# Attention and two MoE layers on one core: operand addresses of the seven products, the order of the raw w_out loads, and which blocks are split on chip

## The chip, the cores and the metric

One core of one Trainium2 chip. The metric is the device time of one execution in microseconds (us), the median over runs. In what follows PE is TensorE (matrix products), PEld its weight loads, DVE is VectorE, ACT is ScalarE, POOL is GpSimd, and SP is SyncE, the engine that issues all DMAs here, in the order of the program.

## The reference, cut to what matters

```python
def _attn_ref(q, k, v, p):              # 8 batches, 8 heads, 576 tokens, 64 columns; p: 32 pack tokens
    p_packed = sm_attn(p, k, v)
    return sm_attn(q, p_packed, p_packed)

def _moe_ref(x, w_gate, w_val, w_out, rms_g):        # 4608 tokens, 512 -> 1536 -> 512
    xn = x / np.sqrt(np.mean(x * x, axis=-1, keepdims=True) + 1e-06) * rms_g
    g = xn @ w_gate
    return (g * (1.0 / (1.0 + np.exp(-g))) * (xn @ w_val)) @ w_out

def _moe2_ref(x, w_in, w_out, alpha):                # 4608 tokens, 512 -> 2048 -> 512
    h = x @ w_in
    return (np.maximum(h, 0.0) + alpha * np.minimum(h, 0.0)) @ w_out
```

The three run one after the other: the output of attention, with the heads side by side, is the x of the first layer, and its output is the x of the second. All tensors are float32.

## The kernel before

Every float32 operand of the large products is split into two parts that TensorE takes at its full rate (fp32r): a high part, made by ACT (`split_hi`, L109), and a low part, the rest, made by DVE (`split_lo`, L112). A product is then three matmuls into the same accumulator (`mm3`, L120 to L123): weights high by moving high (L121), weights high by moving low (L122), weights low by moving high (L123).

The program has two large stages. Until about 940 us, attention and the first layer run in 12 chunks of tokens; the first layer's result goes to y_dram in DRAM. From there on the second layer runs in five groups (`PAIRS`), of widths w = 512, 512, 512, 384 and 384, each covering 2w tokens. The change is to this stage, apart from two of its addresses.

In the second layer, the 2 x 2 block product of tokens by w_in is done with seven products instead of eight. The moving operands are sums and differences of quarters of y, named b11, t1, t2, t4, t3, b21, b22; `prep` (L769) makes them for the next group, in tiles `yh` and `yl` of the pool `p2`. The weights are seven tiles per step, w7, each with a high and a low half. In group 1 they are made on chip (`make_w7`, L824, with ACT and POOL, from raw blocks i2_raw) and stored to w7_dram; groups 2 to 5 load them (`load_w7`, L819, DMA at L822).

A group goes like this:

- Eight steps (the loop over i). Step i has the seven products of six matmuls each. ACT copies the first out as m1 (L1133, a tile `th`), DVE adds the others to it (`add2`, L1033, tiles `tl` and `th`) and applies the PReLU. Then `second` is called for two of the four results, those of the first half of the tokens: hidden blocks i and i + 8. The other two are kept as g2.
- `second` splits the activation into hh and hl, and the w_out block of 128 x 512 into in_h and in_l, by ACT and DVE; then it puts a function that issues the block's matmuls into the list `fill`, from where they are taken later, between the products of the next step. The raw w_out blocks i and i + 8 come from w_dram by one DMA of 512 KB (`load_o2`, L1046 to L1052) into one of two tiles o2_raw, one for even i and one for odd. So the load for step i + 2 can start when DVE has made in_l of block i + 8 of step i. In group 1 the in_h, in_l of blocks 0 to 7 (e = 0) are also stored to os_dram (L1073).
- The deferred loop (over j = 0 to 15), for the second half of the tokens: `second` takes the kept g2, in the order of blocks 0, 8, 1, 9, and so on. Blocks 0 to 7 (j even, `again` and e = 0) are not split: in_h and in_l are loaded from os_dram (L1067). Blocks 8 to 15 (j odd) are split from o2_raw, which is loaded for them with 256 KB each. At j = 2, `results` (L1090) copies the sums of the first half out by ACT and DVE and stores them (DMA at L1101).
- The `results` of the second half are called at the end of step 0 of the next group.

All engines take their instructions in program order, and so does SP with its DMAs: a DMA that has to wait for its tile, or for an evacuation, holds back all DMAs behind it. The w7 tiles of four of the seven products and the in_h, in_l tiles share 12 places of the pool `wa`. In the names of the profile the numbers are dropped, and w7_dram and w_dram both read `w_dram`; a w7 tile is `w`, o2_raw is `o_raw`, i2_raw is `i_raw`.

At L1116 to L1120 a step of before begins (after group 1) with the loads of the weights for the next step, and then with its own raw w_out load:

```python
                elif i + 1 < NP2:
                    load_w7(k_ + 1, EARLY + ORDER)
                elif pr + 1 < len(PAIRS):
                    load_w7(k_ + 1, EARLY)
                load_o2(i)
```

Of the kernel before, what the change touches and what calls it, by code (L numbers as in the profile page):

```python
# [8 lines left out]
F32 = mybir.dt.float32  # L9
# [9 lines left out]
def attention_moe_moe2_kernel(ctx, tc, q, k, v, p, w_gate, w_val, w_out, rms_g, w_in2, w_out2, alpha, out):  # L19
    nc = tc.nc  # L20
# [8 lines left out]
    NF2 = FF2 // 128  # L29
# [5 lines left out]
    NJ = NF // 2  # L35
# [6 lines left out]
    NP2 = NF2 // 2  # L42
    PAIRS, t0_ = [], 0
# [44 lines left out]
    one = ctx.enter_context(tc.tile_pool(name="one", bufs=1))  # L88
    wg1 = ctx.enter_context(tc.tile_pool(name="wg1", bufs=NWG1))
    ps = ctx.enter_context(tc.tile_pool(name="ps", bufs=1, space=bass.MemoryType.PSUM))  # L90
    y_dram = tc.dram_tile([KD, 128, NT], F32, name="y_dram")
    w7_dram = tc.dram_tile([NP2 * 7, 128, 2, 256], F32, name="w7_dram")
    os_dram = tc.dram_tile([NP2, 2, 128, 512], F32, name="os_dram")
    w_dram = tc.dram_tile([2 * NF2, 128, 4, 128], F32, name="w_dram")
    gv_dram = tc.dram_tile([NJ * 4, 128, 512], F32, name="gv_dram")

    ident = const.tile([128, 128], F32, name="ident")
    g_col = const.tile([128, HG], F32, name="g_col")
# [9 lines left out]
    def split_hi(hi, src):  # L108
        nc.scalar.activation(out=hi, in_=src, func=ACTF.Copy)  # L109

    def split_lo(lo, src, hi):
        nc.vector.tensor_tensor(out=lo, in0=src, in1=hi.bitcast(F32), op=ALU.subtract)  # L112
# [7 lines left out]
    def mm3(o, lh, ll, rh, rl, first, last, more=False):  # L120
        nc.tensor.matmul(out=o, lhsT=lh, rhs=rh, start=first, stop=False, skip_group_check=more)  # L121
        nc.tensor.matmul(out=o, lhsT=lh, rhs=rl, start=False, stop=False, skip_group_check=more)  # L122
        nc.tensor.matmul(out=o, lhsT=ll, rhs=rh, start=False, stop=last, skip_group_check=more)  # L123

    with tc.manual_schedule():
# [685 lines left out]
        def new_w7(k_, which):  # L811
            for n in which:
                if n in EARLY:
                    t = one.tile([128, 2, 256], F32R, tag="gv", name="w7", bufs=8)
                else:
                    t = wa.tile([128, 2, 256], F32R, tag="w", name="w7")
                w7[k_, n] = t
# [6 lines left out]
        def make_w7(i):  # L824
            new_w7(i, EARLY + ORDER)
            blocks = []
            for e in range(2):
                t = one.tile([128, 2, 256], F32, tag="s7", name="i2_raw", bufs=2)
                nc.sync.dma_start(
                    out=t.rearrange("p h x -> p (h x)"),  # L830
                    in_=w_dram[2 * (i + e * NP2)].rearrange("p c x -> p (c x)"),
                )
                blocks += [t[:, 0], t[:, 1]]
            a11, a12, a21, a22 = blocks

            def product(n, src):
                t = w7[i, n]
                split_hi(t[:, 0], src)
                nc.gpsimd.tensor_tensor(out=t[:, 1], in0=src, in1=t[:, 0].bitcast(F32), op=ALU.subtract)
                nc.sync.dma_start(out=w7_dram[i * 7 + n], in_=t.bitcast(F32))  # L840

            def combine(out, x, y, op):
                nc.gpsimd.tensor_tensor(out=out, in0=x, in1=y, op=op)

            yield
            product(0, a11)
            product(1, a12)
            product(3, a22)
            combine(a22, a21, a22, ALU.add)
            yield  # L850
            combine(a21, a11, a21, ALU.subtract)
            product(4, a22)
            combine(a11, a22, a11, ALU.subtract)
            yield
            product(6, a21)
            combine(a12, a12, a11, ALU.subtract)
            yield
            product(5, a11)
            product(2, a12)
# [5 lines left out]
        for c, (t0, n, cuts) in enumerate(CH):  # L865
# [148 lines left out]
            if c == NP1 - 2:  # L1014
                ap_ctx.close()
                p2 = ctx.enter_context(tc.tile_pool(name="p2", bufs=1, side="right", reuse_waits="tile"))
# [29 lines left out]
        def load_o2(i, e0=0):  # L1046
            x = "hl"[i % 2]
            t = one.tile([128, 2, T], F32, tag="x" + x, name="o2_raw")
            nc.sync.dma_start(
                out=t[:, e0:2], in_=o2_pair[i, 1, e0:2].rearrange("e p x -> p e x")  # L1050
            )
            o2[i] = t  # L1052
# [3 lines left out]
        def second(g, f, w, acc, first, last, keep=False, again=False):  # L1056
            n_h[0] += 1
            hh, hl = [
                ring.tile([128, T], F32R, tag="ho"[n_h[0] % 2] + x, name="h" + x, bufs=2)[:, 0:w] for x in "hl"
            ]  # L1060
            split_hi(hh, g)
            split_lo(hl, g, hh)
            oh, ol = [wa.tile([128, T], F32R, tag="w", name="in_" + x) for x in "hl"]
            e, i = divmod(f, NP2)
            if again and e == 0:
                for x, t in enumerate((oh, ol)):
                    nc.sync.dma_start(out=t.bitcast(F32), in_=os_dram[i, x])  # L1067
            else:
                split_hi(oh, o2[i][:, e])
                split_lo(ol, o2[i][:, e], oh)  # L1070
            if keep and e == 0:
                for x, t in enumerate((oh, ol)):
                    nc.sync.dma_start(out=os_dram[i, x], in_=t.bitcast(F32))  # L1073

            def block():
                for t in range(w // 128):
                    cs = slice(t * 128, (t + 1) * 128)
                    mm3(acc(t), hh[:, cs], hl[:, cs], oh, ol, first, last)
            fill.append(block)
# [23 lines left out]
                    )  # L1103

        finish = None
        making = make_w7(1)
        next(making)
        for pr, (t0, w) in enumerate(PAIRS):
            odd = pr % 2
            acc1, acc2 = accumulators(1 - odd), accumulators(odd)  # L1110
            g2 = {}
            for i in range(NP2):
                k_ = pr * NP2 + i
                if pr == 0 and i + 1 < NP2:
                    pass
                elif i + 1 < NP2:  # L1116
                    load_w7(k_ + 1, EARLY + ORDER)
                elif pr + 1 < len(PAIRS):
                    load_w7(k_ + 1, EARLY)
                load_o2(i)  # L1120
                if i == NP2 - 2 and pr + 1 < len(PAIRS):
                    y_rows.append(load_rows(pr + 1, 0))

# [45 lines left out]
                    finish()  # L1169
                    finish = None  # L1170
            prepare = prep(pr + 1) if pr + 1 < len(PAIRS) else iter(())
            load_o2(0, 1)
            for j in range(NF2):
                i, e = divmod(j, 2)
                f = i + e * NP2
                if e == 0 and i + 1 < NP2:
                    load_o2(i + 1, 1)
                second(g2[f], f, w, acc2, j == 0, j == NF2 - 1, again=True)
                if len(fill) > 3:
                    fill.pop(0)()  # L1180
                if j == 2:
                    results(acc1, t0, w)
                next(prepare, None)
# [8 lines left out]
        fill.pop(0)()  # L1192
        fill.pop(0)()
        finish()
        nc.gpsimd.memset(p2.tile([128, 8], F32, tag="pad", name="pad"), 0.0)


# [28 lines left out]
```

## Time and profile before

| What | Value |
|---|---|
| time, median of 3 runs (lowest to highest) | 1723.32 us (1721.94 to 1723.66) |
| the profiled execution: time, span | 1730.86 us, 1729.0 us |
| mean granted TensorE clock of the span | 0.973 |
| PE busy | 1629.4 us, 94% |
| PEld busy | 1362.7 us, 79% |
| DVE busy | 1122.6 us, 65% |
| ACT busy | 704.3 us, 41% |
| POOL busy | 355.4 us, 21% |
| DMA | 287.60 MB, mean 166 GB/s |

The span is from the first to the last instruction of the profiled execution; its own time is longer by what lies around the span, 1.9 us. Busy shares are of the span, and over both stages. The granted clock is a share of TensorE's 2.4 GHz: 1.00 is that level, 0.50 the lower one of 1.2 GHz. In the rows further down, a name `out<-in` tells what an instruction writes and reads, and a bracket at a row's end tells how long the engine had stood idle before it and whose result it waited for. Matmuls overlap in the pipeline, so the time from the start of one to the start of the next tells what a matmul costs, and not its own duration.

### The profile page before, as it was taken

To read this page: it belongs to the slowest core of one execution; us is meant where nothing else is said; L and a number is where in the kernel's file an instruction comes from. 1 tells how busy PE (TensorE), PEld (TensorE's weight loads), DVE (VectorE), ACT (ScalarE), POOL (GpSimd) and SP (SyncE) were. 2 spreads that over 40 slices of the span, in tenths; PEclk is the share of its full clock that TensorE was granted. 3 is DMA by queue.
4 is the path that set the end of the run, shared out by engine and by line. 5 is a ranking of instruction groups with operands and counts; after the bars stand their busy time and mean duration, and the time that the engine had idled before them with its cause. 6 is when DMAs were issued, how large, how long until landed. Compare 5 with 4: busy or idle time off the path is not lost.

```text
span 1729.0 us, 28160 instructions
## 1 busy us (share of the span) xinstructions
PE 1629.4 (94%) x10378; PEld 1362.7 (79%) x10378; DVE 1122.6 (65%) x2097; ACT 704.3 (41%) x1517; POOL 355.4 (21%) x321
## 2 busy tenths in 40 slices
PE   6787998999999899999999999999999999999898
PEld 4455787888878888888888787878787878888896
DVE  4766456666565665665558778567756675686673
ACT  3564445555455454545444333321331132133123
POOL 1441122333223323333227551000000000000000
PEclk8798899999999999999999999999999999999999
DMA  8975455735655253542122666565446545656735
GB/s 208 291 219 156 133 148 172 188 81 172 171 168 161 78 159 129 171 123 77 50 86 98 241 224 215 176 208 178 140 157 216 186 140 171 230 170 222 240 125 176
DMA packets 226168, 287.60 MB, mean 166 GB/s; under 512 B 94448, under 2 KB 112880, under 8 KB 226032
## 3 DMA queue, kind: packets, MB, share of 16 engines
q1 hardware_dynamic: 226032, 285.81, 52.6%
q8 instruction: 82, 1.34, 0.3%
q14 instruction: 54, 0.44, 0.1%
HBM read 233.32 MB, written 52.43 MB: 165 GB/s over the span
## 4 chain that ended last, share of the span: by engine, by line
PE 73%; DVE 13%; ACT 5%; DMA 3%; issue 2%; POOL 1%; SPq 0%; DVEq 0%; ACTq 0%; POOLq 0%
PE ps_y L121 11%; PE ps_y L122 10%; PE ps_y L123 10%; PE ps_g L122 10%; PE ps_g L121 10%; PE ps_g L123 10%; PE ps_wg L669 2%; PE ps_v L121 2%; PE ps_v L122 2%; PE ps_v L123 2%; DVE s L979 1%; ACT hh L109 1%; DVE hl L112 1%; DVE s L975 1%; DMA in_l<-os_dram 1%
## 5 line engine op out<-in xcount | busy, mean ns | idle before, releaser
L307 POOL TENSOR_TENSOR in_l<-w_raw,in_h 128x512 fp32r<-128x512 f32 x131 | 172.4, 1316 | 385.0 <-ACT in_h L109 345.0
L121 PE MATMUL ps_y<-hh,in_h 128*128 128x320 f32 (+1 forms) x576 | 208.9, 363 | 5.7 <-ACT hh L109 5.7
L122 PE MATMUL ps_y<-hl,in_h 128*128 128x320 f32 (+1 forms) x576 | 198.2, 344 | 0.6
L123 PE MATMUL ps_y<-hh,in_l 128*128 128x320 f32 (+1 forms) x576 | 197.3, 343 | 0.0
L109 ACT ACTIVATE hh<-tl 128x512 fp32r<-128x512 f32 (+1 forms) x80 | 47.0, 588 | 367.1 <-DVE tl L1040 367.1
L975 DVE SCALAR_TENSOR_TENSOR s<-s,ps_g 128x320 f32<-128x320 f32 (+1 forms) x132 | 71.3, 540 | 156.1 <-ACT s L970 155.8
L109 ACT ACTIVATE hh<-s 128x320 fp32r<-128x320 f32 (+1 forms) x144 | 75.5, 524 | 208.5 <-DVE s L979 208.5
L112 DVE TENSOR_TENSOR hl<-s,hh 128x320 fp32r<-128x320 f32 (+1 forms) x144 | 89.0, 618 | 85.0 <-ACT hh L109 85.0
L121 PEld LDWEIGHTS ps_y<-hh,in_h 128*128 128x128 f32 x576 | 110.9, 193 | 35.5 <-issue 19.5
L121 PE MATMUL ps_g<-yh,w 128*128 128x512 f32 (+1 forms) x336 | 128.5, 383 | 8.1 <-ACT th L1133 8.1
L121 PE MATMUL ps_g<-xh,wgh 128*128 128x256 f32 (+3 forms) x384 | 119.4, 311 | 9.5 <-ACT wgh L109 2.6
L123 PE MATMUL ps_g<-yh,w 128*128 128x512 f32 (+1 forms) x336 | 127.5, 379 | 0.0
L122 PE MATMUL ps_g<-yl,w 128*128 128x512 f32 (+1 forms) x336 | 127.4, 379 | 0.0
L109 ACT ACTIVATE in_h<-w_raw 128x512 fp32r<-128x512 f32 x144 | 90.4, 628 | 87.8 <-PE ps_y L122 84.5
L122 PE MATMUL ps_g<-xl,wgh 128*128 128x256 f32 (+3 forms) x384 | 118.5, 309 | 3.4 <-DVE xl L112 3.3
L123 PE MATMUL ps_g<-xh,wgl 128*128 128x256 f32 (+3 forms) x384 | 117.9, 307 | 0.7 <-DVE wgl L112 0.7
L122 PEld LDWEIGHTS ps_y<-hl,in_h 128*128 128x128 f32 x576 | 111.3, 193 | 8.9 <-DVE hl L112 2.2
L123 PEld LDWEIGHTS ps_y<-hh,in_l 128*128 128x128 f32 x576 | 110.9, 192 | 8.5
L121 PE MATMUL ps_v<-xh,wgh 128*128 128x256 f32 (+3 forms) x384 | 117.2, 305 | 0.0
L122 PE MATMUL ps_v<-xl,wgh 128*128 128x256 f32 (+3 forms) x384 | 116.7, 304 | 0.0
L123 PE MATMUL ps_v<-xh,wgl 128*128 128x256 f32 (+3 forms) x384 | 116.5, 303 | 0.0
L121 PE MATMUL ps_g<-in_h,hh 128*128 128x512 f32 x288 | 113.2, 393 | 2.9 <-DMA in_h<-os_dram 2.1
(184 smaller groups left out, 4045.3 us busy)
## 6 DMA issues: line engine op xcount, KB each, us to landing
w<-w_dram SPq DMA_DIRECT2D x224, 256.0 KB, 4.6
gv_raw<-gv_dram SPq DMA_DIRECT2D x168, 256.0 KB, 3.7
w_dram<-w SPq DMA_DIRECT2D x88, 256.0 KB, 2.2
o_raw<-w_dram SPq DMA_DIRECT2D x40, 512.0 KB, 5.5
w<-in_moe_w_out_dram SPq DMA_DIRECT2D x28, 512.0 KB, 4.3
o_raw<-w_dram SPq DMA_DIRECT2D x40, 256.0 KB, 2.7
in_h<-os_dram SPq DMA_DIRECT2D x40, 256.0 KB, 3.4
in_l<-os_dram SPq DMA_DIRECT2D x40, 256.0 KB, 4.2
```

The costliest lines, as they stand in the source:

```text
L109: nc.scalar.activation(out=hi, in_=src, func=ACTF.Copy)
L112: nc.vector.tensor_tensor(out=lo, in0=src, in1=hi.bitcast(F32), op=ALU.subtract)
L121: nc.tensor.matmul(out=o, lhsT=lh, rhs=rh, start=first, stop=False, skip_group_check=more)
L122: nc.tensor.matmul(out=o, lhsT=lh, rhs=rl, start=False, stop=False, skip_group_check=more)
L123: nc.tensor.matmul(out=o, lhsT=ll, rhs=rh, start=False, stop=last, skip_group_check=more)
L307: nc.gpsimd.tensor_tensor(out=l, in0=raw[u], in1=h.bitcast(F32), op=ALU.subtract)
L669: nc.tensor.matmul(out=ts[g][h * NP:(h + 1) * NP, :], lhsT=ppG[b][e * D:(e + 1) * D, c_, :], rhs=us[c_][e * D:(e + 1) * D, :], start=True, ...
L975: nc.vector.scalar_tensor_tensor(out=s, in0=s, scalar=1.0, in1=tg, op0=ALU.add, op1=ALU.mult)
L979: nc.vector.tensor_tensor(out=s, in0=s, in1=tv, op=ALU.mult)
```

## The change

It has four parts.

1. *Addresses.* i2_raw moves from the pool `one` to the pool `p2`, and the last pad tile of `p2` grows from 8 to 40 floats. With that, the operand tiles of the seven products, yh and yl, start 64 bytes past a multiple of 256 bytes of a partition's memory; before, it was 192 bytes. Their weights, w7, start 64 bytes past one in both. The four DRAM tiles are declared in another order.
2. *Raw w_out blocks a step ahead.* `load_o2(0)` is called before the first group, and step i calls `load_o2(i + 1)`, ahead of its `load_w7`; step 7 calls `load_o2(0)` for the deferred loop, and j = 14 calls it for the next group.
3. *Block 0 of the deferred loop* (j = 0) is split on chip, from the raw tile that step 7 has loaded with both blocks, in every group.
4. *The last group* splits all eight blocks 0 to 7 of its deferred loop on chip; its raw loads there take both blocks (512 KB).

Parts 3 and 4 remove 24 loads from os_dram and add 12 splits, each one ACT and one DVE operation. The number of matmuls, the products and all other splits are the same.

```diff
@@ -89,10 +89,10 @@
     y_dram = tc.dram_tile([KD, 128, NT], F32, name="y_dram")
+    w_dram = tc.dram_tile([2 * NF2, 128, 4, 128], F32, name="w_dram")
+    gv_dram = tc.dram_tile([NJ * 4, 128, 512], F32, name="gv_dram")
     w7_dram = tc.dram_tile([NP2 * 7, 128, 2, 256], F32, name="w7_dram")
     os_dram = tc.dram_tile([NP2, 2, 128, 512], F32, name="os_dram")
-    w_dram = tc.dram_tile([2 * NF2, 128, 4, 128], F32, name="w_dram")
-    gv_dram = tc.dram_tile([NJ * 4, 128, 512], F32, name="gv_dram")
@@ -825,7 +825,7 @@
             for e in range(2):
-                t = one.tile([128, 2, 256], F32, tag="s7", name="i2_raw", bufs=2)
+                t = p2.tile([128, 2, 256], F32, tag="s7", name="i2_raw", bufs=2)
@@ -1062,7 +1062,7 @@
             e, i = divmod(f, NP2)
-            if again and e == 0:
+            if again:
                 for x, t in enumerate((oh, ol)):
                     nc.sync.dma_start(out=t.bitcast(F32), in_=os_dram[i, x])
@@ -1103,6 +1103,7 @@
         finish = None
+        load_o2(0)
         making = make_w7(1)
@@ -1111,13 +1112,17 @@
             for i in range(NP2):
                 k_ = pr * NP2 + i
+                split_late = pr + 1 == len(PAIRS)
+                if i + 1 < NP2:
+                    load_o2(i + 1)
+                else:
+                    load_o2(0)
                 if pr == 0 and i + 1 < NP2:
                     pass
                 elif i + 1 < NP2:
                     load_w7(k_ + 1, EARLY + ORDER)
                 elif pr + 1 < len(PAIRS):
                     load_w7(k_ + 1, EARLY)
-                load_o2(i)
@@ -1169,13 +1174,14 @@
             prepare = prep(pr + 1) if pr + 1 < len(PAIRS) else iter(())
-            load_o2(0, 1)
             for j in range(NF2):
                 i, e = divmod(j, 2)
                 f = i + e * NP2
                 if e == 0 and i + 1 < NP2:
-                    load_o2(i + 1, 1)
-                second(g2[f], f, w, acc2, j == 0, j == NF2 - 1, again=True)
+                    load_o2(i + 1, 0 if split_late else 1)
+                if j == NF2 - 2 and pr + 1 < len(PAIRS):
+                    load_o2(0)
+                second(g2[f], f, w, acc2, j == 0, j == NF2 - 1, again=e == 0 and j > 0 and not split_late)
@@ -1192,7 +1198,7 @@
-        nc.gpsimd.memset(p2.tile([128, 8], F32, tag="pad", name="pad"), 0.0)
+        nc.gpsimd.memset(p2.tile([128, 40], F32, tag="pad", name="pad"), 0.0)
```

**SP, the start of group 2 (steps 0 and 1), before.** `w` is a w7 tile, `o_raw` the raw w_out pair, `stg` a sum of group 1 that goes out.

```order
L822 DMA w_12690<-w_dram 128x512
L1049 DMA o_raw<-w_dram 128x2x512
L1101 DMA out_dram<-stg_12813 128x2x512
L1101 DMA out_dram<-stg_12817 128x2x512
L822 DMA w_12821<-w_dram 128x512
L822 DMA w_12822<-w_dram 128x512
L822 DMA w_12823<-w_dram 128x512
L822 DMA w_12824<-w_dram 128x512
L822 DMA w_12825<-w_dram 128x512
L822 DMA w_12826<-w_dram 128x512
L822 DMA w_12827<-w_dram 128x512
L1049 DMA o_raw<-w_dram 128x2x512
```

The same place with the change:

```order
L1049 DMA o_raw<-w_dram 128x2x512
L822 DMA w_12688<-w_dram 128x512
L822 DMA w_12689<-w_dram 128x512
L822 DMA w_12690<-w_dram 128x512
L822 DMA w_12691<-w_dram 128x512
L822 DMA w_12692<-w_dram 128x512
L822 DMA w_12693<-w_dram 128x512
L822 DMA w_12694<-w_dram 128x512
L1101 DMA out_dram<-stg_12815 128x2x512
L1101 DMA out_dram<-stg_12819 128x2x512
L1049 DMA o_raw<-w_dram 128x2x512
L822 DMA w_12825<-w_dram 128x512
```

The raw pair of step 1 stood behind the two stores and seven w7 loads; now it stands ahead of the w7 loads of step 0 and of the stores, and that of step 2 stands behind the stores and ahead of the w7 loads.

**SP, the start of the deferred loop of group 2, before.** `in_h` and `in_l` are the split blocks that are loaded.

```order
L822 DMA w_13603<-w_dram 128x512
L822 DMA w_13604<-w_dram 128x512
L822 DMA w_13605<-w_dram 128x512
L1049 DMA o_raw<-w_dram 128x2x512
L1049 DMA o_raw<-w_dram 128x512 x2
L1067 DMA in_h<-os_dram 128x512
L1067 DMA in_l<-os_dram 128x512
L1049 DMA o_raw<-w_dram 128x512
```

And with the change:

```order
L1049 DMA o_raw<-w_dram 128x2x512
L822 DMA w_13607<-w_dram 128x512
L822 DMA w_13608<-w_dram 128x512
L822 DMA w_13609<-w_dram 128x512
L1049 DMA o_raw<-w_dram 128x512 x2
L1067 DMA in_h<-os_dram 128x512
L1067 DMA in_l<-os_dram 128x512
L1101 DMA out_dram<-stg_13790 128x2x512
```

The first in_h, in_l of before were those of block 0; those of the change are of block 1 (j = 2), behind the raw loads of steps j = 2 and j = 4.

**DVE, the start of the deferred loop of group 5, before.** `hl` is the low part of an activation, `in_l` that of a w_out block.

```order
L112 TENSOR_TENSOR hl<-tl,hh 128x384
L112 TENSOR_TENSOR in_l<-o_raw,in_h 128x512
L112 TENSOR_TENSOR hl<-g_17089,hh 128x384
L112 TENSOR_TENSOR hl<-g_17083,hh 128x384
L112 TENSOR_TENSOR in_l<-o_raw,in_h 128x512
L112 TENSOR_TENSOR hl<-g_17222,hh 128x384
L118 COPY stg_18035<-ps_y_17202 128x512
```

And with the change:

```order
L112 TENSOR_TENSOR hl<-tl,hh 128x384
L112 TENSOR_TENSOR in_l<-o_raw,in_h 128x512
L112 TENSOR_TENSOR hl<-g_17091,hh 128x384
L112 TENSOR_TENSOR in_l<-o_raw,in_h 128x512
L112 TENSOR_TENSOR hl<-g_17085,hh 128x384
L112 TENSOR_TENSOR in_l<-o_raw,in_h 128x512
L112 TENSOR_TENSOR hl<-g_17224,hh 128x384
L112 TENSOR_TENSOR in_l<-o_raw,in_h 128x512
L118 COPY stg_18035<-ps_y_17204 128x512
```

Each even block of the loop has a split of its own now; in groups 1 to 4 this holds for the first alone.

## Rows read from the trace of the kernel before

**Rows 1.** Waits of PE, 985 to 1729 us: total us, times, longest us.

```profile
PE ps_g L121 <- ACT th L1133: 5.5, 3, 4.0
PE ps_y L121 <- DVE tl L1033: 3.5, 2, 2.9
PE ps_y L121 <- ACT th L1133: 2.6, 2, 1.3
PE ps_g L122 <- DMA in_l<-os_dram: 2.1, 3, 0.8
PE ps_g L121 <- DMA in_h<-os_dram: 2.1, 2, 1.5
PE ps_y L121 <- DMA in_h<-os_dram: 1.3, 1, 1.3
PE ps_y L122 <- DMA in_l<-os_dram: 1.3, 2, 0.7
PE ps_y L121 <- ACT stg L116: 0.6, 1, 0.6
PE ps_g L121 <- ACT stg L116: 0.6, 1, 0.6
```

**Rows 2.** PE in time order, steps 2 and 1 of groups 4, 5: start, duration (us).

```profile
1473.92 0.33 PE L123 MATMUL ps_y<-yh,w 128*128 128x384 f32 x1
1477.18 0.44 PE L121 MATMUL ps_y<-yh,w 128*128 128x384 f32 x1 [2.93 <-DVE tl L1033]
...
1600.08 0.44 PE L121 MATMUL ps_g<-yh,w 128*128 128x384 f32 x1 [0.51 <-ACT th L1133]
```

**Rows 3.** ACT in time order, at the start of step 2 of group 4.

```profile
1475.31 0.63 ACT L109 ACTIVATE in_h<-o_raw 128x512 fp32r<-128x512 f32 x1 [8.57 <-DMA o_raw<-w_dram]
```

**Rows 4.** SP's queue in time order, steps 0 and 1 of group 4.

```profile
1448.37 0.42 SPq L1049 DMA_DIRECT2D o_raw<-w_dram  x1
1463.53 0.98 SPq L1101 DMA_DIRECT2D out_dram<-stg  x2
1464.56 4.51 SPq L822 DMA_DIRECT2D w<-w_dram  x7
1469.12 0.43 SPq L1049 DMA_DIRECT2D o_raw<-w_dram  x1
```

**Rows 5.** Windows: us, engines busy (instructions), clock, DMA share, GB/s; group 4.

```profile
1480.20:1482.44 2.24, 2.24 (x8) 2.24 (x8) 0.67 (x2) 0.00 (x0) 0.00 (x0) 0.50 0.88 323
```

**Rows 6.** PE in time order, start of the deferred loop of group 4.

```profile
1553.56 0.47 PE L121 MATMUL ps_y<-in_h,hh 128*128 128x512 f32 x1 [1.32 <-DMA in_h<-os_dram]
1554.71 0.79 PE L122 MATMUL ps_y<-in_l,hh 128*128 128x512 f32 x1 [0.68 <-DMA in_l<-os_dram]
```

**Rows 7.** SP's queue in time order, start of the deferred loop of group 4.

```profile
1551.02 0.38 SPq L1067 DMA_DIRECT2D in_l<-os_dram  x1
...
1553.50 0.38 SPq L1067 DMA_DIRECT2D in_l<-os_dram  x1
```

**Rows 8.** DVE in time order, end of step 0 of group 4.

```profile
1462.17 0.69 DVE L112 TENSOR_TENSOR in_l<-o_raw,in_h 128x512 fp32r<-128x512 f32 x1
```

**Rows 9.** PE in time order, products of group 1 and of group 4.

```profile
1049.64 0.40 PE L122 MATMUL ps_g<-yl,w 128*128 128x512 f32 x1
...
1054.08 0.39 PE L123 MATMUL ps_g<-yh,w 128*128 128x512 f32 x1
...
1471.99 0.34 PE L121 MATMUL ps_y<-yh,w 128*128 128x384 f32 x1
```

**Rows 10.** PE in time order, w_out matmuls of group 2's deferred loop.

```profile
1230.81 0.39 PE L121 MATMUL ps_g<-in_h,hh 128*128 128x512 f32 x1
...
1235.35 0.39 PE L123 MATMUL ps_g<-in_h,hl 128*128 128x512 f32 x1
```

**Rows 11.** PE in time order, gate and value products of the first layer.

```profile
277.64 0.31 PE L121 MATMUL ps_g<-xh,wgh 128*128 128x320 f32 x1
...
279.25 0.31 PE L123 MATMUL ps_v<-xh,wgl 128*128 128x320 f32 x1
```

## The prediction

> **What bounds the kernel now.** I read the share of busy time first (the table above): PE is busy nearly all of the span, so a gain must come from holes in PE's work or from a shorter matmul. Next I read who PE waited for in the last stage, from group 2 on [rows 1]. What the reader is to see there: the idle time falls into two sorts. The first three rows are waits for `th` (the copy m1, L1133) and `tl` (an addition, L1033): 5.5 + 2.6 + 3.5 = 11.6 us. The others are waits for in_h and in_l from os_dram, 2.1 + 2.1 + 1.3 + 1.3 us, with two of 0.6 that are put down to an evacuation of ACT: 8.0 us in ten waits. These two of 0.6 stand at the same instruction as the in_h waits of the other groups (the first matmul of a deferred block); the ACT result that this matmul needs was long there, so I take them for the same DMA.
>
> Then I looked where they stand. The first sort stands at the start of step 2 of groups 2 to 5 [rows 2]; one of its waits, 0.5 us, is another matter (the row at 1600.08: m1 stands behind the evacuations of `results`). Going back from there: ACT's split of the raw w_out block waited 8.6 us for its DMA [rows 3]. That DMA was issued late [rows 4]: SP stands at the out_dram store of the group before from 1448.8 to 1463.5, then issues seven w7 loads, and only then, at 1469.12, the o2 load, which is there 6.1 us later. ACT is in order, so everything behind the split (the splits of the second block and m1) is late, and PE with it. The second sort stands at the start of the deferred loop [rows 6]: SP issues the os_dram load of block 0 late [rows 7], because it stands behind the raw load that waits for DVE's last split of the step before.
>
> What such a wait costs is more than the idle time shown. From 1473.92 to 1477.18 PE starts nothing for 3.26 us where two products follow each other after 0.18; 3.08 are lost, against 2.93 shown, and the first matmul behind the wait takes 0.44 instead of 0.33: in all 0.26 more than the idle time. In groups 4 and 5 the granted clock falls after the wait to 0.50, the lower level (1.2 GHz); a product of 384 columns then takes 2.24 / 7 = 0.32 us instead of 0.175 [rows 5].
>
> **The change part by part.**
>
> *The raw blocks one step ahead.* In the queue of SP the o2 load of step i + 1 now stands ahead of the w7 loads of step i, so that of step 1 is issued in step 0, ahead of the store at which SP waits. The 8.6 us wait of ACT goes, and with it PE's: 11.6 - 0.5 = 11.1 us idle, six waits at 0.26 make 1.6, and some 21 products at the lower clock (ten in group 4, eleven in group 5) at 0.145 make 3.0: **15.7 us**. What is late next there is m1 behind the evacuations, 0.5 us in group 5, which stays. The new order has a price: the load waits for DVE's split of step i - 1, and seven w7 loads now stand behind it. In the rows that split ends at 1462.86 [rows 8], before SP came free in any case; in a usual step it ends near the step's own start. I cost this at nothing: the w7 tiles are for step i + 1, and a step of 384 columns takes 42 x 0.175 + 18 x 0.227 = 11.4 us. If that cover is gone, it is the second rival.
>
> *Block 0 of the deferred loop split on chip, and all of them in group 5.* The os_dram loads of j = 0 go in all groups; o2 block 0 is there already. The ten waits go: 8.0 + 10 x 0.26 = 10.6 us, and in groups 4 and 5 some seven matmuls each at the lower clock, where 512 columns take 0.2 us more, 2.8: 13.4 us. Added are 12 splits, each one ACT operation of some 0.6 us (the 0.63 in [rows 3] is one) and one DVE operation of 0.69 [rows 8]; they lie beside PE's blocks (12 x 0.227 = 2.7 us, or 2.05 in a group of 384). But on DVE the one of block 0 stands ahead of that of block 1, and the raw load of j = 2 waits for the latter, with the os_dram loads of j = 2 behind it. In group 4 the last of these is issued at 1553.50 [rows 7]; now 0.7 later, at 1554.2. The one issued at 1551.02 was there at 1554.71, 3.7 us later [rows 6, 7], so this one lands at 1557.9. PE, which now starts block 0 at 1553.56 - 1.32 - 0.16 = 1552.08, wants it two blocks and one matmul later, at 1556.4: a new wait of 1.5 us. In groups 1 to 3 the two blocks are 1.36 us longer, which leaves 0.1 each. In group 5 there are no os_dram loads; the raw load of 512 KB has two blocks of time and I put it at 0, at most 1. Net **13.4 - 1.8 = 11.6 us**.
>
> *The operands of the seven products.* In the program as built the operand tiles yh, yl start 192 bytes past a multiple of 256, and all other moving operands of mm3 and all its weights 64 bytes past one; now these start at 64 too. No row of before has both kinds for one instruction, so I bound it by neighbours. A product of 512 columns takes (1054.08 - 1049.64) / 19 = 233.7 ns from start to start, and one of 384 (1473.92 - 1471.99) / 11 = 175.5 [rows 2, 9]. At the granted clock of 1.00 the columns alone are 213.3 and 160.0, so the rest is 20.4 and 15.5 ns. The w_out matmuls of the same stage take (1235.35 - 1230.81) / 20 = 227.0 [rows 10], a rest of 13.7; those of the stage before with xh take (279.25 - 277.64) / 11 = 146.4 at 320 columns [rows 11], a rest of 13.1, though they too put six in a row into one bank. So with the same start the rest seems fixed at some 13.4, and the products could save 6.7 ns x 1008 + 2.1 ns x 672 = **8.1 us**. Lower bound 0, as the start address need not be the cause; I take the full value, since the one kind that differs in address is the one that is slow. The Trainium skill (TensorE: Matmul & The Clock Gate, Back-to-back issue gap and the part on LDWEIGHTS behind it) speaks against this: it gives N / 2.4 + 2.5 ns whatever the addresses, and two independent read ports for weights and moving operand; by it the sum would be without the 8.1. The trace does not bear out its 215.8 ns at 512 columns: the rows have 227.0 and 233.7.
>
> *The rest.* The order of the DRAM tiles, the place of i2_raw and the larger pad move addresses only; no row shows that a DMA's time depends on them, and I put them at 0. The first group's own waits for m1 (before 985 us) hang on GpSimd's making of w7, which stays.
>
> **The sum.** 15.7 + 11.6 + 8.1 = 35.4 us. The profiled execution took 1730.9 us, so 1695.5 there; the median of the runs shown is 7.6 us lower, and by it I forecast **1687.9 us**. Should all of these 7.6 us be waits that only the profile has, the gain would be 27.8 and the time 1695.5.
>
> **The rivals.**
> 1. The addresses do nothing, and that part of the change does not do what it says: the slow pitch of the products would belong to something else that they have alone (w7 tiles with both halves in one tile, or their waits for tiles). For it: no row has the cure. Against it: six in a row into one bank, weights written by DMA and many waits occur among the fast ones too. The products keep 233.7 ns, and the time is 1687.9 + 8.1 = **1696.0 us**. This is what the page of the Trainium skill just cited would have.
> 2. **Slower:** the w7 loads come late. SP stands in every step at the o2 load; from there the seven w7 issues take 4.5 us and a 512 KB load lies ahead of them. If the last is there later than one step after SP came free (11.4 us in a group of 384), PE waits in every step. With the longest landing seen here, 6.1 us, the last is there 0.4 + 4.5 + 6.1 = 11.0 us after, and PE needs the first ones at the step's end, the last some 6 us on. It decides only if landings grow by 5 us. Fourteen steps of groups 4 and 5 with 3 us each would make 42 us: **1730 us**.
> 3. The deferred loop comes to hang on its os_dram loads: PE gets ahead, and the loads of j = 2 and j = 4 are late in each of groups 1 to 4, eight waits of 1.5 us in place of the 1.8 counted: **1698.1 us**.
> 4. Both new orders give back what they win (o2 load and deferred loads each late by as much as before), and the addresses do nothing: no change.
>
> **How the numbers follow.** Forecast 0.57, rival 1 0.25, rival 3 0.11, rival 2 0.05, rival 4 0.02. About 0.2%, 3.4 us, is what a measurement of this kernel can tell from no change. Faster: 0.57 + 0.25 + 0.11 = 0.93; same 0.02; slower 0.05. The range goes down to 1684 (no new wait in group 4, 1.8; the 0.8 us at 1600.08 with its restart; 1 us more at the matmuls just behind the products), and up to 1702: rival 1 with four new waits of 1.5 us.
>
> **What would show it.** Right: ACT's wait for o_raw gone from step 1 of groups 2 to 5, no PE wait for `tl`, and for `th` only the short one; no wait for os_dram at j = 0, one of about 1.5 us at j = 2 of group 4, none in group 5; granted clock 1.00 from 1069 us on; products 227 ns apart at 512 columns and 173 at 384. Products still at 233 are rival 1. Waits of the products for w7 loads are rival 2. Waits of L121 or L122 for os_dram in most groups are rival 3. Wrong altogether if PE's idle time in the last stage stays near 20 us under other names.

## The result, and the profile after

The change takes **1695.62 us** (median of 6 runs, 1693.40 to 1697.54) beside 1723.28 us of the kernel before (6 runs): ratio 0.984, 95% interval 0.9827 to 0.9852. It is 27.7 us faster; the forecast was 1687.9, the range 1684 to 1702. Its profiled execution took 1693.40 us, span 1691.6, mean granted clock 0.980.

The shares of busy time of the change: PE's share rises by one point only, since PE had few holes before.

```profile
PE 1610.1 (95%) x10378; PEld 1353.6 (80%) x10378; DVE 1129.2 (67%) x2109; ACT 708.5 (42%) x1529; POOL 356.0 (21%) x321
```

What PE waited for in the change from 985 us on (total us, times, longest us), beside [rows 1]:

```profile
PE ps_y L121 <- ACT in_h L109: 1.2, 2, 0.9
PE ps_g L121 <- ACT th L1138: 0.5, 1, 0.5
PE ps_g L121 <- ACT in_h L109: 0.3, 1, 0.3
PE ps_y L121 <- DMA in_h<-os_dram: 0.2, 1, 0.2
PE ps_g L122 <- DVE in_l L112: 0.2, 1, 0.2
PE ps_y L122 <- DVE in_l L112: 0.2, 1, 0.2
```

The waits for `tl` are gone, of those for `th` only the 0.5 us behind the evacuations is left, and of the ten waits for os_dram two: that of 0.2, and one of 0.9 that the view puts down to ACT's in_h, though it is for such a load too (shown below). In all PE waits 2.6 us; before, the waits in this window came to 20.6, those of 0.3 us and less included.

SP's queue of the change at steps 0 and 1 of group 4 answers to [rows 4], ACT's split of the first raw block of step 1 to [rows 3], PE at the start of step 2 to [rows 2], and the window from 1066 us to the end to [rows 5] (columns as there):

```profile
1424.26 0.37 SPq L1049 DMA_DIRECT2D o_raw<-w_dram  x1
```

```profile
1446.76 0.61 ACT L109 ACTIVATE in_h<-o_raw 128x512 fp32r<-128x512 f32 x1
```

```profile
1455.10 0.33 PE L123 MATMUL ps_y<-yh,w 128*128 128x384 f32 x1
1455.28 0.33 PE L121 MATMUL ps_y<-yh,w 128*128 128x384 f32 x1
```

```profile
1066.00:1691.00 625.00, 618.78 (x2862) 527.03 (x2860) 441.96 (x769) 186.91 (x356) 0.00 (x0) 1.00 0.54 188
```

The raw pair of step 1, issued at 1469.12 before, is now issued at 1424.26, in step 0, and its split at 1446.76 waits for nothing. Where PE started nothing for 3.26 us, the next matmul now starts after 0.18; the clock stays at 1.00. The products of group 1, a run of 30 from its first to its last:

```profile
1040.78 0.39 PE L121 MATMUL ps_g<-yh,w 128*128 128x512 f32 x1
...
1047.36 0.39 PE L123 MATMUL ps_g<-yh,w 128*128 128x512 f32 x1
```

(1047.36 - 1040.78) / 29 = 226.9 ns from start to start, against 233.7 in [rows 9] and 227.0 for the w_out matmuls [rows 10].

### The profile page after: what moved, and what is told of

The parts are those of the page before. It is cut to its first block, busy times and chain, and to the rows that moved or that the text cites. A ratio compares the mean times of both kernels' runs of the same rounds, so it can differ in the third digit from the quotient of the medians.

```text
span 1691.6 us, 28163 instructions
## 1 busy us (share of the span) xinstructions
PE 1610.1 (95%) x10378; PEld 1353.6 (80%) x10378; DVE 1129.2 (67%) x2109; ACT 708.5 (42%) x1529; POOL 356.0 (21%) x321
## 4 chain that ended last, share of the span: by engine, by line
PE 74%; DVE 13%; ACT 4%; issue 2%; DMA 2%; POOL 1%; SPq 1%; DVEq 0%; ACTq 0%; POOLq 0%
PE ps_y L121 11%; PE ps_y L122 10%; PE ps_y L123 10%; PE ps_g L122 10%; PE ps_g L123 10%; PE ps_g L121 10%; PE ps_wg L669 2%; PE ps_v L121 2%; PE ps_v L122 2%; PE ps_v L123 2%; DVE s L979 2%; DVE hl L112 1%; ACT hh L109 1%; DVE s L975 1%; DVE yl L112 1%
## 5 line engine op out<-in xcount | busy, mean ns | idle before, releaser
L121 PE MATMUL ps_g<-yh,w 128*128 128x512 f32 (+1 forms) x336 | 125.3, 373 | 4.4 <-ACT th L1138 4.4
L123 PE MATMUL ps_g<-yh,w 128*128 128x512 f32 (+1 forms) x336 | 124.8, 372 | 0.0
L122 PEld LDWEIGHTS ps_y<-hl,in_h 128*128 128x128 f32 x576 | 111.3, 193 | 8.9 <-DVE hl L112 2.2
L121 PE MATMUL ps_y<-in_h,hh 128*128 128x512 f32 x288 | 112.3, 390 | 1.4 <-ACT in_h L109 1.2
```

## The experiments

The stage before the last is the same code in all kernels here, yet the last stage begins between 932.6 and 937.8 us. So beside the time of a run I give the length of its *last stage* in its trace: from the start of the first product to the start of the last matmul. In the change this is 1687.52 - 933.22 = 754.3 us.

| Run | Median us (runs) | Ratio to before, 95% interval | Last stage, us |
|---|---|---|---|
| before, first profile | 1723.28 (6) | | 787.2 |
| before_again | 1723.08 (1) | | 783.6 |
| addr_only | 1719.82 (8) | 0.9972, 0.9962 to 0.9982 | 778.0 |
| ahead_only | 1711.46 (5) | 0.9931, 0.9919 to 0.9944 | 769.7 |
| no_addr | 1700.06 (4) | 0.9863, 0.9848 to 0.9878 | 760.4 |
| no_addr_again | 1701.11 (4) | 0.9873, 0.9859 to 0.9886 | 762.5 |
| the change | 1695.62 (6) | 0.984, 0.9827 to 0.9852 | 754.3 |
| change_again | 1694.17 (4) | 0.9832, 0.9818 to 0.9846 | 754.9 |
| left_192 | 1699.53 (1) | | 761.0 |
| all_192 | 1697.07 (1) | | 755.5 |
| y_at_128 | 1697.84 (1) | | 758.9 |
| y_at_0 | 1701.30 (1) | | 761.9 |
| w7_raw_first | 1693.79 (5) | 0.9831, 0.9817 to 0.9844 | 752.9 |
| os_first | 1691.67 (4) | 0.9825, 0.9807 to 0.9843 | 751.7 |

The ratios are to the kernel before on the same occasion: 1723.87 us (12 runs) for before_again to no_addr, 1723.12 us (9 runs) for change_again, no_addr_again, w7_raw_first and os_first. The four runs on addresses were taken once, beside one of the kernel before at 1727.53 us, for their start to start times.

### Where the first profile's 7.6 us lay

before_again is the kernel before with an empty line at its end.

> The kernel before, unchanged, profiled once more: its first profile took 1730.9 us where six timed runs took 1721.9 to 1723.7, and the two traces differ by 37.5 us, 4.5 of them before 219 us, in code that is the same. Theory A: the 7.6 us that the first profile had over the median lie in the waits that the change removes (start of step 2 of groups 2 to 5, start of the deferred loops), so that these cost some 24 us in place of 32 here, and the last stage begins near 938 us. Theory B: they lie elsewhere, 4.5 us in the first 219 us; then the last stage begins near 933 us, and the waits cost 32 us again.

It took 1723.08 us, 7.8 less than the first profile. The first product of the last stage, in the trace of before and in that of before_again:

```profile
937.78 0.49 PE L121 MATMUL ps_g<-yh,w 128*128 128x512 f32 x1
```

```profile
933.03 0.49 PE L121 MATMUL ps_g<-yh,w 128*128 128x512 f32 x1
```

So 4.8 of the 7.8 us lie ahead of the stage that the change is about, as theory B has it. The last stage is 3.6 us shorter (787.2 to 783.6); what follows its last matmul is 0.6 longer.

Most of these 3.6 us lie in group 1. The copy m1 of its last step starts 111.7 us behind the first product in the first profile, and 109.3 in before_again:

```profile
1049.47 0.58 ACT L1133 ACTIVATE th<-ps_g 128x512 f32<-128x512 f32 x1
```

```profile
1042.33 0.58 ACT L1133 ACTIVATE th<-ps_g 128x512 f32<-128x512 f32 x1
```

In between PE waits for m1 twice, 0.7 and 1.8 us in the first profile, 0.7 and 1.0 in before_again. Behind the wait of 1.8 us the mean granted clock is 0.61 from 973.5 to 977.0 us; in before_again it stays at 1.00.

```profile
973.58 0.50 PE L121 MATMUL ps_g<-yh,w 128*128 128x512 f32 x1 [1.82 <-ACT th L1133]
```

The starts of the copies m1 part the whole last stage in this way (us; sums over the groups; two numbers are the run and its repeat; differences in the text are taken before rounding):

| Stretch | before, first profile | before_again | ahead_only | no_addr | the change |
|---|---|---|---|---|---|
| group 1, first product to m1 of step 7 | 111.7 | 109.3 | 111.3 | 111.5, 111.8 | 109.8, 109.7 |
| around step 2: m1 of step 1 to m1 of step 3, groups 2 to 5 | 120.4 | 121.9 | 104.7 | 104.7, 104.7 | 103.6, 103.7 |
| deferred loops: m1 of step 7 to m1 of the next step 0, or to the last matmul | 279.9 | 277.1 | 278.4 | 269.1, 270.8 | 268.4, 269.0 |
| the rest | 275.2 | 275.2 | 275.2 | 275.2, 275.2 | 272.5, 272.5 |

The waits that the change removes stand in the second and third rows. There the first profile is 1.6 us shorter than before_again and 2.8 longer, 1.2 us longer in all. So theory B holds for all but 1.2 us.

### The parts one by one

addr_only is the kernel before with part 1 of the change without the DRAM order:

```diff
-                t = one.tile([128, 2, 256], F32, tag="s7", name="i2_raw", bufs=2)
+                t = p2.tile([128, 2, 256], F32, tag="s7", name="i2_raw", bufs=2)
-        nc.gpsimd.memset(p2.tile([128, 8], F32, tag="pad", name="pad"), 0.0)
+        nc.gpsimd.memset(p2.tile([128, 40], F32, tag="pad", name="pad"), 0.0)
```

> Only the addresses of the operands of the seven products (i2_raw in p2, the pad of 40 floats). In the trace after the change a product of 512 columns takes 226.9 ns from start to start in place of 232.9, one of 384 some 174.9 in place of 175.9. If the address is the cause: 1008 x 5.9 + 672 x 1.0 = 6.6 us, 1716.7 us, the products at 227 and 173 to 175. If the pitch came with the other two parts (fewer waits, other loads beside the products): no change, 1723.3 us, and 233 ns.

The first and the last of the 30 products of group 1:

```profile
1038.73 0.39 PE L121 MATMUL ps_g<-yh,w 128*128 128x512 f32 x1
...
1045.31 0.39 PE L123 MATMUL ps_g<-yh,w 128*128 128x512 f32 x1
```

They take 6.58 / 29 = 0.2269 us each, 227 ns at 512 columns, so the address is the cause, and none of the other parts. The last stage is 5.6 us shorter; the time fell by 4.0 us, with an interval of 3.1 to 6.6 that has the expected 6.6 at its end. Its PE waits from 985 us on sum up to 19.2 us, against 18.5 in before_again. Whether the shorter products always wait a little longer at the late loads, these runs don't settle.

ahead_only is the change with that diff undone, and with the deferred loop of before:

```diff
-                    load_o2(i + 1, 0 if split_late else 1)
+                    load_o2(i + 1, 1)
-                second(..., again=e == 0 and j > 0 and not split_late)
+                second(..., again=e == 0)
```

> Only the raw w_out blocks a step ahead: addresses as before, all blocks of e = 0 of the deferred loops from os_dram. The waits at the start of step 2 of groups 2 to 5 cost 15.6 us in the trace of before (2.5, 1.3, 6.1, 5.7). Theory A (part of the 7.6 us lie there): 8 to 12 us, 1711 to 1715 us. Theory B: 15.6 us, 1707.7 us. In both no PE wait for tl, the waits for os_dram at the start of the deferred loops stay (10 to 16 us) and the products stay at 233 ns.

12.4 us less (interval 9.7 to 14.0), 13.9 in the last stage, between the two theories. PE's waits from 985 us on in ahead_only:

```profile
PE ps_g L121 <- DMA in_h<-os_dram: 2.6, 3, 1.3
PE ps_y L121 <- DMA in_h<-os_dram: 1.3, 1, 1.3
PE ps_y L122 <- DMA in_l<-os_dram: 1.0, 2, 0.6
PE ps_g L122 <- DMA in_l<-os_dram: 0.8, 2, 0.5
PE ps_y L121 <- ACT stg L116: 0.6, 1, 0.6
PE ps_g L121 <- ACT th L1138: 0.5, 1, 0.5
```

All waits at step 2 are gone, so the mechanism is right; the waits for os_dram stay, as both theories said. By the table of stretches the one around step 2 is 17.2 us shorter than in before_again (15.7 than in the first profile); 2.0 of it are given back in group 1, of which more below, and 1.3 in the deferred loops.

no_addr is the change with part 1 undone, DRAM order kept (the first diff here, with its signs reversed).

> The change without its addresses: raw blocks ahead and the splits on chip, operands of the products at 192 bytes past a multiple of 256 again. If the address is the cause of the slow products: 6.6 us more than the change, 1702.2 us, products at 233 ns. If not: 1695.6 us, and 227 ns. Against ahead_only it shows the splits alone: 10.6 us by the traces (16.6 us of waits at the start of the deferred loops before, 6.0 after).

1700.06 us: the splits are worth 1711.46 - 1700.06 = 11.4 us (9.3 and 7.2 in the last stage of the two executions profiled), and the products are back at 233.1 ns (30 of group 1 start between 1041.98 and 1048.74). Since the change had been timed on another occasion, both were run again side by side:

> The change, unchanged, as the measure for the other three on this chip: 1693 to 1698 us.

> The change without its addresses once more, beside the change: by the start to start times of the products 6.6 us above it. If the products' gain is partly eaten by waits that do not move (loads that come at the same time whatever PE does), only 4 to 5 us, as in the first comparison.

1701.11 - 1694.17 = 6.9 us, the whole of what the start to start times say (6.6); the second theory falls here. Timed, the three parts add up to 30.7 us, 12.4, 11.4 and 6.9; the whole change is 27.7 us below the kernel before in one set of runs and 29.0 in the other. So the parts are known to some 2 us, not to a tenth.

### Which addresses make a product slow

Each is the change with one or two pads altered. The pool of yh, yl lies at the other end of the memory than the rest, so the two pads move the two sides apart.

```diff
# left_192
-    pad0 = const.tile([128, 8], F32, name="pad0")
+    pad0 = const.tile([128, 40], F32, name="pad0")
# all_192: as left_192, and
-        nc.gpsimd.memset(p2.tile([128, 40], F32, tag="pad", name="pad"), 0.0)
+        nc.gpsimd.memset(p2.tile([128, 8], F32, tag="pad", name="pad"), 0.0)
# y_at_128: [128, 24] in place of [128, 40]; y_at_0: [128, 56]
```

> The change with all tiles but those of the pool with yh, yl (y_raw, w7, in_h, in_l, hh, hl, xh and so on) moved by 128 bytes, to 192 past a multiple of 256; yh, yl stay at 64. Theory R (a matmul is slow where moving operand and weights start differently): products at 233 ns again though yh, yl stand at 64, w_out matmuls at 227; 6.6 us above the change. Theory A (a moving operand that starts at 192 is slow, whatever the weights): products at 227 ns, w_out matmuls of the last stage (in_h, in_l at 192) at 233, 1728 x 5.9 = 10 us above the change there, and the first layer slower too.

> The change with everything at 192 bytes past a multiple of 256, yh, yl too. Theory R: nothing differs between operands, products and w_out matmuls at 227 ns, time as the change's, 1693 to 1698 us. Theory A: both at 233 ns, some 17 us more in the last stage alone.

> The change with yh, yl at 128 past a multiple of 256 (pad of 24 floats), all else at 64. Theory R, any difference counts: products at 233 ns or more. Theory R, only a difference of 128 counts: 227. Theory A: says only that 192 is slow; 227 if 128 is well placed.

> The change with yh, yl at a multiple of 256 (pad of 56 floats), all else at 64. Theory R, any difference: products at 233 ns. If a start at a multiple of 128 or 256 were the best there is, whatever the weights: below 227 or at 227.

PE in order of time, the first and the last of 30 products of group 1, in left_192, and of 68 w_out matmuls of its deferred loop:

```profile
1041.51 0.40 PE L121 MATMUL ps_g<-yh,w 128*128 128x512 f32 x1
...
1048.27 0.39 PE L123 MATMUL ps_g<-yh,w 128*128 128x512 f32 x1
...
1084.72 0.39 PE L122 MATMUL ps_g<-in_l,hh 128*128 128x512 f32 x1
...
1099.91 0.39 PE L123 MATMUL ps_g<-in_h,hl 128*128 128x512 f32 x1
```

The same 30 products in all_192, in y_at_128 and in y_at_0:

```profile
1043.54 0.39 PE L121 MATMUL ps_g<-yh,w 128*128 128x512 f32 x1
...
1050.11 0.39 PE L123 MATMUL ps_g<-yh,w 128*128 128x512 f32 x1
```

```profile
1042.09 0.40 PE L121 MATMUL ps_g<-yh,w 128*128 128x512 f32 x1
...
1048.75 0.39 PE L123 MATMUL ps_g<-yh,w 128*128 128x512 f32 x1
```

```profile
1042.88 0.40 PE L121 MATMUL ps_g<-yh,w 128*128 128x512 f32 x1
...
1049.64 0.40 PE L123 MATMUL ps_g<-yh,w 128*128 128x512 f32 x1
```

The last column is the mean start to start time over the 384-column products of groups 4 and 5, those over 300 ns left out.

| Run | yh, yl past a multiple of 256 | w7 past one | 512 columns, ns | 384 columns, ns |
|---|---|---|---|---|
| the change | 64 | 64 | 226.9 | 174.9 |
| all_192 | 192 | 192 | 226.6 | 174.9 |
| y_at_128 | 128 | 64 | 229.7 | 173.8 |
| y_at_0 | 0 | 64 | 233.1 | 176.9 |
| no_addr | 192 | 64 | 233.1 | 175.8 |
| left_192 | 64 | 192 | 233.1 | 175.8 |

left_192 and all_192 settle it for theory R: yh, yl at 64 are slow when their weights stand at 192, and at 192 fast when these do too; so are the w_out matmuls of left_192 with both operands at 192, (1099.91 - 1084.72) / 67 = 226.7. What counts is how far apart the moving operand and the weights start; why, no run here shows. It isn't all or nothing: 64 bytes above costs 2.8 ns, 64 below 6.2. Other distances, and whether the weights of the same or of the next matmul count, weren't tried.

### What the change left, and two repairs

Before 985 us the new order makes the first w7 tiles late. In group 1, SP's queue, ACT and PE, in before_again:

```profile
933.56 0.91 SPq L829 DMA_DIRECT2D i_raw<-w_dram  x2
...
936.91 1.02 ACT L109 ACTIVATE w<-i_raw 128x256 fp32r<-128x256 f32 x3
...
951.49 0.50 PE L121 MATMUL ps_g<-yh,w 128*128 128x512 f32 x1 [0.72 <-ACT th L1133]
```

and in the change:

```profile
933.80 0.37 SPq L1049 DMA_DIRECT2D o_raw<-w_dram  x1
934.23 0.97 SPq L829 DMA_DIRECT2D i_raw<-w_dram  x2
...
938.94 1.08 ACT L109 ACTIVATE w<-i_raw 128x256 fp32r<-128x256 f32 x3 [1.74 <-DMA i_raw<-w_dram]
...
953.33 0.50 PE L121 MATMUL ps_g<-yh,w 128*128 128x512 f32 x1 [2.58 <-ACT th L1138]
```

The 512 KB of raw w_out stand ahead of i2_raw, from which w7 is made. ACT's first splits of it are 2.0 us later (938.94 against 936.91), and PE's first wait for m1, which stands behind them on ACT, is 1.9 us longer. In change_again the wait of 2.3 us there is followed by the lower clock as well:

```profile
953.80:957.20 3.40, 3.16 (x8) 2.49 (x9) 1.30 (x3) 0.93 (x4) 0.25 (x1) 0.54 0.94 300
```

w7_raw_first puts group 1 back:

```diff
-        load_o2(0)
         making = make_w7(1)
...
-                if i + 1 < NP2:
-                    load_o2(i + 1)
-                else:
+                if pr == 0:
+                    load_o2(i)
+                if i + 1 == NP2:
                     load_o2(0)
+                elif pr > 0:
+                    load_o2(i + 1)
```

> The change, but in group 1 the raw w_out blocks are loaded as before (i2_raw for the making of w7 ahead of them), a step ahead only from its last step on. Theory: the w_out load ahead of i2_raw made the first w7 some 2 us late, so that the waits of PE for m1 between 945 and 975 us cost 3.0 to 4.5 us in the runs with the new order, 2.2 to 3.0 in those with the old. Then about 2 us less than the change and these waits at 2 to 3 us. Rival (these waits hang on POOL alone and differ by chance): no difference.

PE's first wait for m1 is 0.88 us again:

```profile
951.01 0.50 PE L121 MATMUL ps_g<-yh,w 128*128 128x512 f32 x1 [0.88 <-ACT th L1139]
```

So the order is the cause of that wait. But the next one is 1.44 (1.30 in the change, none in change_again), and the time, 1693.79, can't be told from change_again's 1694.17. The last stage is 1.4 to 2.0 us shorter, and the stretch of group 1 in the table above takes 108.3 us where the change has 109.8 and 109.7; but os_first below has the same order there and takes 110.1. So that the repair wins time is not shown.

In the deferred loop of group 4 the change has two waits, at j = 2 and at j = 4. PE in order of time:

```profile
1530.08 0.39 PE L123 MATMUL ps_y<-in_h,hl 128*128 128x512 f32 x1
1530.70 0.47 PE L121 MATMUL ps_y<-in_h,hh 128*128 128x512 f32 x1 [0.24 <-DMA in_h<-os_dram]
1531.28 0.50 PE L122 MATMUL ps_y<-in_l,hh 128*128 128x512 f32 x1
1531.62 0.40 PE L123 MATMUL ps_y<-in_h,hl 128*128 128x512 f32 x1
...
1535.04 0.39 PE L123 MATMUL ps_y<-in_h,hl 128*128 128x512 f32 x1
1536.34 0.47 PE L121 MATMUL ps_y<-in_h,hh 128*128 128x512 f32 x1 [0.91 <-ACT in_h L109]
```

Against 0.227 a step, the three starts from 1530.08 to 1531.62 lose 0.86 us; the second wait loses 1.07 and, with its next two matmuls, 1.5. The view puts the second wait down to ACT's in_h, but it is for a load from os_dram. A block has nine matmuls here; the loop starts at 1526.22, and 36 matmuls lie ahead of the wait, so it stands at the fifth block, j = 4, which isn't split on chip. Its in_h is issued at 1531.75, behind the raw load that could go only when DVE's split of j = 3, begun at 1530.62, was done, and lands at 1536.20, 0.14 us ahead of the matmul:

```profile
1531.33 0.33 SPq L1049 DMA_DIRECT2D o_raw<-w_dram  x1
1531.75 0.51 SPq L1067 DMA_DIRECT2D in_h<-os_dram  x1
```

In change_again the same wait, at the same block, carries its right name:

```profile
1537.94 0.47 PE L121 MATMUL ps_y<-in_h,hh 128*128 128x512 f32 x1 [0.33 <-DMA in_h<-os_dram]
```

os_first is w7_raw_first with the two calls of the deferred loop exchanged:

```diff
+                second(g2[f], f, w, acc2, j == 0, j == NF2 - 1, again=...)
                 if e == 0 and i + 1 < NP2:
                     load_o2(i + 1, 0 if split_late else 1)
                 if j == NF2 - 2 and pr + 1 < len(PAIRS):
                     load_o2(0)
-                second(g2[f], f, w, acc2, j == 0, j == NF2 - 1, again=...)
```

> As w7_raw_first, and in the deferred loops the os_dram loads of block i stand ahead of the raw load of step i + 1. If the wait for os_dram at j = 2 of group 4 (0.9 us with its restart) comes from standing behind the raw load: gone, 0.9 us less than w7_raw_first. If the raw load is then later and the wait for the split of a raw block at j = 5 of group 4 (1.5 us) grows by as much: no difference.

PE's waits from 985 us on in os_first:

```profile
PE ps_g L121 <- ACT th L1139: 0.5, 1, 0.5
PE ps_g L121 <- ACT in_h L109: 0.3, 1, 0.3
PE ps_y L121 <- ACT in_h L109: 0.3, 1, 0.3
PE ps_y L122 <- DVE in_l L112: 0.2, 1, 0.2
PE ps_g L122 <- DVE in_l L112: 0.2, 1, 0.2
```

Both waits are gone: both loads had stood behind a raw load. The expectation took the second for a wait on the split of a raw block, at j = 5, and so counted 0.9 us; the deferred loops take 265.4 us where w7_raw_first has 268.4, and the last stage is the shortest of all, though its waits in group 1 were long this time. Its median of 1691.67 us is the lowest, 2.5 below change_again's, with overlapping intervals: the best version tried, not shown to be faster than the change.

## Why the prediction was right, and where it was off

**Faster, in the range, and 7.7 us less of it than forecast.** The sum, 35.4 us, stands beside 37.5 between the two first profiles (1730.86 - 1693.40), but 4.6 of these lie ahead of the last stage, where the change does nothing; the medians show 27.7. The text had the other reading too ("the gain would be 27.8 and the time 1695.5") and did not choose it. That its number comes out is luck: it asks that all 7.6 us be waits that only the profile has, and before_again shows 1.2 us in the stretches that were costed and the rest elsewhere. So it isn't the median that failed, but terms of the sum. From before_again to the change (mean of its two traces) the last stage is 29.0 us shorter. Without the addresses (no_addr, mean of two) the stretch around step 2 gives 17.3 and the deferred loops 7.2, group 1 is 2.3 longer: together 22.1 where 27.3 was forecast. The addresses give 6.9 where 8.1 was forecast.

**Raw blocks ahead: 15.7 forecast, 12.4 timed, 13.9 in the traces.** The waits named are gone, the clock stays up, and what was late next was m1 behind the evacuations, 0.5 us, as said; the stretch around step 2 is shorter by the 15.7 of the forecast against the first profile, and by 17.2 against before_again. What failed is "The first group's own waits for m1 (before 985 us) hang on GpSimd's making of w7, which stays": the making starts from i2_raw, and the change puts 512 KB ahead of that load. A queue that a moved load passes was followed for groups 2 to 5, and not for group 1. Its first wait for m1 is 1.9 us longer in the change than in before_again. What this costs in all is open: group 1 takes 111.3 to 111.8 us with the new order and the old addresses, but with the old order it takes 109.3 in one execution of the kernel before and 111.7 in the other.

**Splits on chip: 11.6 forecast, 11.4 timed, 8.2 in the traces.** No wait at j = 0, none in group 5, one at j = 2 of group 4 for os_dram: forecast with 1.5 us, measured 0.86, since the load was there after 3.1 us (1528.21 to the matmul at 1531.28) in place of 3.7. The load that it hangs on was issued at the time worked out (1528.21 in the profile, which is 1554.2 less the 26 us by which group 4 ends its steps earlier). Not counted was the wait at j = 4, 1.5 us, again for a load that stands behind a raw load: what rival 3 has for groups 1 to 4 came in one of them. Together 2.4 against 1.8. Of the 3.4 us that are missing in the traces, 1.5 lie on the side of before: the 11.6 were read off the first profile, whose deferred loops take 279.9 us, and those of ahead_only take 278.4. Another 1.6 lie on the side of after: 279.9 - 11.6 = 268.3 was forecast, and no_addr has 269.1 and 270.8, with one more late load in group 3 (0.7 us) in the second.

**Addresses: 8.1 forecast, 6.9 timed and 6.9 in the traces.** That the operands' start is the cause was right (rival 1, with a quarter of the chance, falls). The size was off since the rest of 13.4 ns was taken for all widths: 512 columns gained 6.2 of the 6.7 ns, 384 only 0.9 of 2.1. And the reason was half right: it is not how the moving operand starts, but how it starts against its weights.

The Trainium skill (TensorE: Matmul & The Clock Gate, Step-by-step: what each phase is for, under LDWEIGHTS) has weights and moving operand on two independent read ports, so that loading the next weights takes no read bandwidth from the running matmul. The runs show that the two are not without effect on each other: with the same instructions, 6.2 ns of 233.1 hang on where the one starts against the other. Whether it is their reads that meet, no run shows.

**Rivals 2, 3 and 4.** No product waited for a w7 tile in the window from 985 us on, so rival 2 has nothing; of rival 3's eight waits there are two, at j = 2 and j = 4 of group 4; rival 4 falls with the result.

## What to carry to other kernels

Before a sum is taken off the median, find out where the profiled run's own surplus over the median lies; here 4.8 of 7.8 us were in a stage that the change doesn't touch and 2.4 in waits that it doesn't remove, and a second profile of the same kernel showed that. And read the costs off both profiles: the deferred loops alone differ by 2.8 us. Before a wait is taken for what the view names, count which block it stands at and look when the loads of that block landed. When a load is moved ahead in an in-order queue, follow it through every stage that shares the queue, the first one too, where other loads start a chain of their own. And where a matmul's start to start time lies a few ns above that of its neighbours, look at the start addresses of both its operands against each other.

## What was not expected of the hardware

- The start of the moving operand and that of the weights count together: 226.6 to 226.9 ns at 512 columns where both are 64 or both 192 bytes past a multiple of 256, 229.7 with the moving operand 64 bytes above, 233.1 with it 64 below or 128 apart, in either order. At 384 columns the order differs: 173.8 with it 64 above, 174.9 at the same start.
- One kernel's profiled executions differ by 4.8 us in a stage of identical instructions (937.8 and 933.0 us to the first product), and by 2.4 us in group 1 of the next.
- A wait of 2.58 us in group 1 left the granted clock at 1.00 in the change, and one of 2.3 us at the same place was followed by a stretch at 0.54 in change_again; in the first profile of before one of 1.82 us was followed by a stretch at 0.61.
